# Two engines instead of one for emptying PSUM in a SiLU MLP kernel, with a new row order of x and a regrouped end

## Chip, cores, metric

The kernel runs on one core of a Trainium2 chip. The metric is the device time of one execution in microseconds (us); the times below are of several executions of the same program, and the profile is of one execution.

## The reference

```python
B, S, D, F = 1, 2048, 640, 1728     # all bf16
def reference(x, w1, w2):
    h = jnp.einsum("bsd,df->bsf", x, w1)
    h = _silu(h)                     # h * sigmoid(h)
    out = jnp.einsum("bsf,fd->bsd", h, w2)
    return out
```

Two matrix products with a SiLU between them: 2048 rows of x, 640 wide, are taken to 1728 hidden columns and back to 640.

## The kernel before

**Tiling.** Both products contract over the partitions. The 640 columns of x are five blocks of 128 (`DT`), the 1728 hidden columns are padded to fourteen blocks of 128 (`FT`), and the 2048 rows are four chunks of 512 (`NSC`) in the first product and sixteen tiles of 128 (`ST`) in the second. The kernel is written engine by engine: each engine has its own program, in the order in which it will run, and semaphores tie them together. There is no scheduler; the order is what stands there.

**The start.** The first product needs x transposed, as `xT_sb` (columns of x on partitions). For rows 512 to 2047 a transposing DMA does it (L146). For the first chunk TensorE does it: SP loads four pieces of 128 rows into `x0_sb`, one DMA each (L129), with a semaphore each; TensorE multiplies each 128x128 block with an identity (L198, five matmuls for each piece) into PSUM `ps2`, seen as 128-column slots (`tp_view`); VectorE copies the five blocks of a piece, 640 columns, as one cast into `xT_sb` (L282). PSUM holds two pieces, so the transposes of the third piece wait until VectorE has copied the first (`sem_tpc`, L195). While x is under way, TensorE runs four matmuls on zeros (L184), and ScalarE loads its table with a first Sigmoid on a small tile (L258). SP's queue in order: four x pieces, three groups of w1 (L136; the first of them holds two hidden blocks), then a wait for the first w1 group, then fifteen transposing DMAs with w2's loads among them, then the sixteen stores of the output.

**First product (L223).** For each chunk and each hidden block five matmuls with 512 moving columns go into one of four PSUM buffers `ps1`. ScalarE takes the Sigmoid of it into `sig_sb` (L269), VectorE multiplies the two into `hT_sb` (L292), and that frees the buffer. All 56 blocks run before the second product begins.

**Second product (L246).** For each tile of 128 rows, fourteen hidden blocks, and for each of them two matmuls with the same weights (`hT_sb`): 512 output columns into one PSUM bank and 128 into the next. Every matmul has a weight load of its own. `ps2` holds two tiles, so tile st waits for the evacuation of tile st-2 (`sem_ev2`). VectorE casts the 640 columns of a tile into one of three `o_sb` buffers (L305), and SP stores it (L173). At the end SP waits for the stores (L178).

Of the kernel before, what the change touches and what calls it, by code (L numbers as in the profile page):

```python
# [9 lines left out]
def bass_standalone__dense_activation_silu__prompt_kernel(  # L10
# [11 lines left out]
    S, D = xf.shape  # L22
    F = w1.shape[1]
    P = 128
    assert D % P == 0 and S % 512 == 0
    DT = D // P
    FT = (F + P - 1) // P
    FP = FT * P
# [1 line left out]
    ST = S // P  # L30
# [2 lines left out]
    JB = SCH // P  # L33
    NB1 = 4
    NOB = 3
    d_chunks = []
    d0 = 0
    while d0 < D:
        d1 = min(d0 + 512, D)
        d_chunks.append((d0, d1))  # L40
        d0 = d1

    def msz(ft):
        return P

    w1_groups = [(0, 2), (2, 8), (8, FT)]

# [8 lines left out]
    n_w2_dmas = 3 if n_w2_full != FT else 2  # L56
    N_INIT = 4 if FP != F else 3
    N_WARM_MM = 4

    with ExitStack() as es:  # L60
        def sb(name, shape, dtype):
# [22 lines left out]
        sem_init = sem("sem_init")  # L84
        sem_w2pad = sem("sem_w2pad")
        sem_z = sem("sem_z")
        sem_x0 = [sem(f"sem_x0_{j}") for j in range(JB)]
        sem_x = [None] + [sem(f"sem_x{i}") for i in range(1, NSC)]
        sem_w1 = [sem(f"sem_w1_{i}") for i in range(len(w1_groups))]
        sem_w2 = sem("sem_w2")  # L90
        sem_o = [sem(f"sem_o{i}") for i in range(NOB)]
        sem_tp = sem("sem_tp")
        sem_tpc = sem("sem_tpc")
        sem_pe1 = sem("sem_pe1")
        sem_act1 = sem("sem_act1")
        sem_dve1 = sem("sem_dve1")
        sem_pe2 = sem("sem_pe2")
        sem_ev2 = sem("sem_ev2")
        block = es.enter_context(nc.Block())

        w1_v = w1.rearrange("(dt p) f -> p dt f", p=P)
        w2_full_v = w2[0:n_w2_full * P, :].rearrange("(ft p) d -> p ft d", p=P)

        @block.gpsimd
        def _(pool):
# [18 lines left out]

        @block.sync
        def _(sp):
            x0_v = xf[0:SCH, :].rearrange("(j p) d -> p j d", p=P)
            for j in range(JB):
                sp.dma_start(  # L129
                    out=x0_sb[:, j, :], in_=x0_v[:, j, :]  # L130
                ).then_inc(sem_x0[j], 16)

            def load_w1_group(gi):
                a, b = w1_groups[gi]
                f0, f1 = a * P, min(b * P, F)
                sp.dma_start(  # L136
                    out=w1_sb[:, :, f0:f1], in_=w1_v[:, :, f0:f1]
                ).then_inc(sem_w1[gi], 16)

            for gi in range(len(w1_groups)):  # L140
                load_w1_group(gi)

            def x_chunk_transposes(sc):
                s0 = sc * SCH
                for dt in range(DT):
                    sp.dma_start_transpose(  # L146
                        out=xT_sb[:, dt, s0:s0 + SCH],
                        in_=xf[s0:s0 + SCH, dt * P:(dt + 1) * P],
                    ).then_inc(sem_x[sc], 16)

            sp.wait_ge(sem_w1[0], 16)
            for sc in range(1, NSC):
                x_chunk_transposes(sc)
                if sc == min(2, NSC - 1):
                    sp.dma_start(
                        out=w2_sb[:, 0:w2_half, :], in_=w2_full_v[:, 0:w2_half, :]
                    ).then_inc(sem_w2, 16)
                    sp.dma_start(
                        out=w2_sb[:, w2_half:n_w2_full, :],
                        in_=w2_full_v[:, w2_half:n_w2_full, :],  # L160
                    ).then_inc(sem_w2, 16)
                    sp.wait_ge(sem_w2pad, 1)
                    if n_w2_full != FT:
                        sp.dma_start(
                            out=w2_sb[0:F_LAST, FT - 1, :],
                            in_=w2[n_w2_full * P:F, :],
                        ).then_inc(sem_w2, 16)

            o_cnt = [0] * NOB
            for st in range(ST):  # L170
                ob = st % NOB
                sp.wait_ge(sem_ev2, st + 1)
                sp.dma_start(  # L173
                    out=of[st * P:(st + 1) * P, :], in_=o_sb[:, ob, :]
                ).then_inc(sem_o[ob], 16)
                o_cnt[ob] += 1
            for ob in range(NOB):
                sp.wait_ge(sem_o[ob], 16 * o_cnt[ob])  # L178

        @block.tensor  # L180
        def _(pe):
# [8 lines left out]
                )  # L190
            pe.wait_ge(sem_init, N_INIT)
            for j in range(JB):
                pe.wait_ge(sem_x0[j], 16)
                if j >= 2:
                    pe.wait_ge(sem_tpc, j - 1)  # L195
                base = 8 * (j % 2)
                for dt in range(DT):
                    ins = pe.matmul(  # L198
                        tp_view[:, base + dt, :],
                        lhsT=x0_sb[:, j, dt * P:(dt + 1) * P],  # L200
                        rhs=ident[:, :],
                        start=True,
                        stop=True,
                    )
                ins.then_inc(sem_tp, 1)

            w1_waited = set()
            for sc in range(NSC):
                if sc == 0:
                    pe.wait_ge(sem_tpc, JB)  # L210
                else:
                    pe.wait_ge(sem_x[sc], 16 * DT)
                for ft in range(FT):
                    idx = sc * FT + ft
                    buf = idx % NB1
                    gi = w1_group_of(ft)
                    if gi not in w1_waited:
                        pe.wait_ge(sem_w1[gi], 16)
                        w1_waited.add(gi)
                    if idx >= NB1:  # L220
                        pe.wait_ge(sem_dve1, idx - NB1 + 1)
                    for dt in range(DT):
                        ins = pe.matmul(  # L223
                            ps1[:, buf, :],
                            lhsT=w1_sb[:, dt, ft * P:(ft + 1) * P],
                            rhs=xT_sb[:, dt, sc * SCH:(sc + 1) * SCH],
                            start=(dt == 0),
                            stop=(dt == DT - 1),
                        )
                    ins.then_inc(sem_pe1, 1)  # L230
# [1 line left out]
            pe.wait_ge(sem_w2pad, 1)  # L232
            pe.wait_ge(sem_w2, 16 * n_w2_dmas)
            dve1_waited = 0
            for st in range(ST):
                b2 = st % 2
                sc = (st * P) // SCH
                if st >= 2:
                    pe.wait_ge(sem_ev2, st - 1)
                for ft in range(FT):  # L240
                    idx = sc * FT + ft
                    if dve1_waited < idx + 1:
                        pe.wait_ge(sem_dve1, idx + 1)
                        dve1_waited = idx + 1
                    for ci, (c0, c1) in enumerate(d_chunks):
                        ins = pe.matmul(  # L246
                            ps2[:, b2, ci * 512:ci * 512 + (c1 - c0)],
                            lhsT=hT_sb[:, ft, st * P:(st + 1) * P],
                            rhs=w2_sb[:, ft, c0:c1],
                            start=(ft == 0),  # L250
                            stop=(ft == FT - 1),
                        )
                ins.then_inc(sem_pe2, 1)

        @block.scalar
        def _(act):
            act.wait_ge(sem_init, N_INIT)
            act.activation(  # L258
                out=warm_sb[:, :], in_=warm_sb[:, :], func=ACT.Sigmoid
            )  # L260
            for sc in range(NSC):
                for ft in range(FT):
                    idx = sc * FT + ft
                    buf = idx % NB1
                    m = msz(ft)
                    act.wait_ge(sem_pe1, idx + 1)
                    if idx >= NB1:
                        act.wait_ge(sem_dve1, idx - NB1 + 1)
                    act.activation(  # L269
                        out=sig_sb[0:m, buf, :],  # L270
                        in_=ps1[0:m, buf, :],
                        func=ACT.Sigmoid,
                    ).then_inc(sem_act1, 1)

        @block.vector
        def _(dve):
            dve.memset(z_sb[:, :], 0.0).then_inc(sem_z, 1)  # L277
            dve.wait_ge(sem_init, N_INIT)
            for j in range(JB):
                base = 8 * (j % 2)  # L280
                dve.wait_ge(sem_tp, j + 1)
                dve.tensor_copy(  # L282
                    out=xT_sb[:, :, j * P:(j + 1) * P],
                    in_=tp_view[:, base:base + DT, :],
                ).then_inc(sem_tpc, 1)
            for sc in range(NSC):
                for ft in range(FT):
                    idx = sc * FT + ft
                    buf = idx % NB1
                    m = msz(ft)  # L290
                    dve.wait_ge(sem_act1, idx + 1)
                    dve.tensor_tensor(  # L292
                        out=hT_sb[0:m, ft, sc * SCH:(sc + 1) * SCH],
                        in0=ps1[0:m, buf, :],
                        in1=sig_sb[0:m, buf, :],
                        op=ALU.mult,
                    ).then_inc(sem_dve1, 1)
            o_cnt = [0] * NOB
            for st in range(ST):
                b2 = st % 2  # L300
                ob = st % NOB
                dve.wait_ge(sem_pe2, st + 1)
                if o_cnt[ob] > 0:
                    dve.wait_ge(sem_o[ob], 16 * o_cnt[ob])
                dve.tensor_copy(  # L305
                    out=o_sb[:, ob, :], in_=ps2[:, b2, 0:D]
                ).then_inc(sem_ev2, 1)
                o_cnt[ob] += 1


# [26 lines left out]
```

## Time and profile before

| | |
|---|---|
| Median of 6 runs | 135.99 us (134.99 to 136.43) |
| Profiled execution | 136.62 us |
| its span, first to last instruction | 134.7 us |
| First product on the chain (L223) | 46.8% of the span |
| Second product on the chain (L246) | 44.8% |
| DMA of the first w1 group on the chain | 3.5% |
| Issues of the x pieces on the chain (L129) | 1.2% |
| Last evacuation on the chain (L305) | 0.6% |

The span is shorter than the execution's time by 1.9 us, which lie before the first and after the last instruction. In the profile PE is TensorE's matmuls, PEld its weight loads, DVE VectorE, ACT ScalarE, POOL GpSimd, SP the engine that issues all DMAs here; L129 is line 129 of the kernel. The chain is followed back from the last instruction: at each step to what released it, or else to the instruction before it on its engine. In a group of instructions stand how often it ran, its busy time in us, the mean length of one in ns, then how long the engine was idle just before such an instruction and what ended that. In a timeline the first column is the start from the beginning of the span, the second the time until the end of the group, both in us. Some matmul records are missing from a trace.

### The profile page before, as it was taken

Reading aid. Unit: us, or ns where it says so; the run is one execution under the profiler, and the core shown is the slowest. Engines: PE = TensorE matmul, PEld = TensorE weight load, DVE = VectorE, ACT = ScalarE, POOL = GpSimd, SP = SyncE. Lnnn points to the kernel's source line nnn. Section 1 sums busy time; section 2 is a strip of 40 time slices with the busy share of each in tenths; the row PEclk is TensorE's granted clock in tenths of the full one; section 3 lists DMA queues with packets and bytes.
Section 4 is the critical chain, followed back from the end, with each engine's and each line's share of the span. In section 5 each row is a group of like instructions: output and inputs, shape, how many; then the busy total and the mean of one; then the engine's idle time right before and its main releaser. Section 6 shows DMA issues by size and latency. Waiting matters only on the chain.

```text
span 134.7 us, 1780 instructions
## 1 busy us (share of the span) xinstructions
PE 127.9 (95%) x737; PEld 64.8 (48%) x752; DVE 55.2 (41%) x77; ACT 35.0 (26%) x58; POOL 1.6 (1%) x9
## 2 busy tenths in 40 slices
PE   5779999999999999999999999999999999999990
PEld 1523444444444444444445555555555555555550
DVE  0714566666666666666663222221112222221122
ACT  4002555555555555555551000000000000000000
POOL 4000000000000000000000000000000000000000
PEclk9999999999999999999999999999999999999999
DMA  3999446997000000000000110011111110111111
GB/s 114 286 356 233 106 107 164 379 206 147 0 0 0 2 5 0 2 0 0 0 0 0 54 49 25 24 49 54 49 49 49 49 54 14 35 49 49 53 49 49
DMA packets 14792, 9.78 MB, mean 73 GB/s; under 512 B 8576, under 2 KB 14784, under 8 KB 14784
## 3 DMA queue, kind: packets, MB, share of 16 engines
q1 hardware_dynamic: 14784, 9.67, 26.8%
q8 instruction: 6, 0.10, 0.4%
q14 instruction: 2, 0.02, 0.0%
HBM read 5.08 MB, written 2.62 MB: 57 GB/s over the span
## 4 chain that ended last, share of the span: by engine, by line
PE 92%; DMA 4%; SPq 1%; issue 1%; DVE 1%
PE ps L223 47%; PE ps L246 45%; DMA w_sb<-in_w_dram 4%; SPq L129 1%; DVE o_sb L305 1%
## 5 line engine op out<-in xcount | busy, mean ns | idle before, releaser
L223 PE MATMUL ps<-xT_sb,w_sb 128*128 128x512 bf16 x274 | 63.0, 391 | 1.4 <-DMA w_sb<-in_w_dram 1.1
L246 PE MATMUL ps<-w_sb,hT_sb 128*128 128x512 bf16 (+1 forms) x439 | 60.5, 297 | 0.5
L292 DVE TENSOR_TENSOR hT_sb<-ps,sig_sb 128x512 bf16<-128x512 f32 x56 | 38.7, 690 | 26.2 <-ACT sig_sb L269 26.2
L246 PEld LDWEIGHTS ps<-w_sb,hT_sb 128*128 128x128 bf16 x448 | 34.5, 98 | 26.6
L223 PEld LDWEIGHTS ps<-xT_sb,w_sb 128*128 128x128 bf16 x280 | 28.0, 100 | 36.2 <-issue 3.6
L269 ACT ACTIVATE sig_sb<-ps 128x512 bf16<-128x512 f32 x56 | 33.4, 597 | 35.7 <-PE ps L223 35.7
L305 DVE CAST o_sb<-ps 128x640 bf16<-128x640 f32 x16 | 13.2, 825 | 47.2 <-PE ps L246 47.2
L282 DVE CAST xT_sb<-ps 128x640 bf16<-128x640 f32 x4 | 3.1, 820 | 3.0 <-PE ps L198 2.9
L198 PE MATMUL ps<-ident,x_sb 128*128 128x128 bf16 x20 | 2.6, 305 | 0.7 <-DVE xT_sb L282 0.5
L184 PE MATMUL ps<-z_sb 128*128 128x512 bf16 x4 | 1.9, 628 | 1.2 <-DVE z_sb L277 1.2
L198 PEld LDWEIGHTS ps<-ident,x_sb 128*128 128x128 bf16 x20 | 1.9, 135 | 2.1 <-issue 1.3
L258 ACT ACT_TABLE_LOAD x1 | 1.3, 1283 | 0.7 <-PEq L322 0.7
L184 PEld LDWEIGHTS ps<-z_sb 128*128 128x128 bf16 x4 | 0.4, 130 | 1.7 <-DVE z_sb L277 1.2
L121 POOL MEMSET w_sb<- 128x640 bf16 x1 | 0.6, 633 | 0.0
L277 DVE MEMSET z_sb<- 128x256 uint32 x1 | 0.3, 272 | 0.9 <-PEq L322 0.9
L118 POOL MEMSET w_sb<- 128x320 bf16 x1 | 0.4, 367 | 0.0
L108 POOL TENSOR_SCALAR_AFFINE_SELECT ident<-ident 128x128 bf16<-128x128 bf16 x1 | 0.3, 294 | 0.2 <-POOL ident L106 0.2
L258 ACT ACTIVATE warm_sb<-warm_sb 128x32 f32<-128x32 f32 x1 | 0.2, 229 | 0.0
L106 POOL MEMSET ident<- 128x128 bf16 x1 | 0.2, 205 | 0.3 <-POOLq L322 0.3
L119 POOL MEMSET warm_sb<- 128x32 f32 x1 | 0.1, 127 | 0.0
L322 POOL MEMSET const-bfloat16-1.0<- 128x1 bf16 x1 | 0.1, 102 | 0.0
L322 POOL MEMSET const-uint8-127<- 128x1 uint8 x1 | 0.1, 102 | 0.0
(2 smaller groups left out, 0.2 us busy)
## 6 DMA issues: line engine op xcount, KB each, us to landing
out_dram<-o_sb SPq DMA_DIRECT2D x16, 160.0 KB, 1.8
w_sb<-in_w_dram SPq DMA_DIRECT2D x2, 960.0 KB, 6.2
w_sb<-in_w_dram SPq DMA_DIRECT2D x1, 1120.0 KB, 9.3
w_sb<-in_w_dram SPq DMA_DIRECT2D x1, 880.0 KB, 8.6
x_sb<-in_x_dram SPq DMA_DIRECT2D x4, 160.0 KB, 2.6
w_sb<-in_w_dram SPq DMA_DIRECT2D x1, 320.0 KB, 4.7
xT_sb<-in_x_dram SPq DMA_TRANSPOSE x15, 3.5
w_sb<-in_w_dram SPq DMA_DIRECT2D x1, 80.0 KB, 8.9
```

Source lines behind the costliest of these rows:

```text
L118: pool.memset(w1_sb[:, :, F:FP], 0.0).then_inc(sem_init, 1)
L121: pool.memset(w2_sb[:, FT - 1, :], 0.0).then_inc(sem_w2pad, 1)
L129: sp.dma_start(out=x0_sb[:, j, :], in_=x0_v[:, j, :]).then_inc(sem_x0[j], 16)
L184: pe.matmul(ps1[:, NB1 - 1, :], lhsT=z_sb[:, 0:P], rhs=z_sb[:, :], start=True, stop=True,)
L198: ins = pe.matmul(tp_view[:, base + dt, :], lhsT=x0_sb[:, j, dt * P:(dt + 1) * P], rhs=ident[:, :], start=True, stop=True,)
L223: ins = pe.matmul(ps1[:, buf, :], lhsT=w1_sb[:, dt, ft * P:(ft + 1) * P], rhs=xT_sb[:, dt, sc * SCH:(sc + 1) * SCH], start=(dt == 0), stop ...
L246: ins = pe.matmul(ps2[:, b2, ci * 512:ci * 512 + (c1 - c0)], lhsT=hT_sb[:, ft, st * P:(st + 1) * P], rhs=w2_sb[:, ft, c0:c1], start=(ft == 0),
L258: act.activation(out=warm_sb[:, :], in_=warm_sb[:, :], func=ACT.Sigmoid)
L269: act.activation(out=sig_sb[0:m, buf, :], in_=ps1[0:m, buf, :], func=ACT.Sigmoid,).then_inc(sem_act1, 1)
L282: dve.tensor_copy(out=xT_sb[:, :, j * P:(j + 1) * P], in_=tp_view[:, base:base + DT, :],).then_inc(sem_tpc, 1)
L292: dve.tensor_tensor(out=hT_sb[0:m, ft, sc * SCH:(sc + 1) * SCH], in0=ps1[0:m, buf, :], in1=sig_sb[0:m, buf, :], op=ALU.mult,).then_inc(sem ...
L305: dve.tensor_copy(out=o_sb[:, ob, :], in_=ps2[:, b2, 0:D]).then_inc(sem_ev2, 1)
```

## The change

Four things are changed together.

- *x pieces.* Two DMAs of two rows a partition each instead of four of one: row 4p+j of the chunk is now on partition p in piece j, so one DMA reads two neighbouring rows (2560 bytes) for each partition.
- *Transposes.* The five blocks of a piece lie in two PSUM banks, three and two. VectorE copies three (384 columns), ScalarE two (256 columns), each into every fourth column of `xT_sb`, which restores the order of the rows. The semaphore `sem_tpc` becomes two, and TensorE waits for both.
- *Output evacuation.* VectorE copies columns 0 to 511 of a tile, ScalarE columns 512 to 639, each with its own semaphore; TensorE and SP wait for both.
- *The last two tiles.* Their matmuls are regrouped: first both tiles' 512-column halves, 28 matmuls into the two banks of one buffer, then both tiles' 128-column parts, 28 matmuls into the two banks of the other. Each group's evacuations begin when the whole group is done, and each part has its own store: four stores in place of two.

```diff
+    DA = 512
+    DB = D - DA
...
+    TPV = 3
+    def tp_slot(j, dt):
+        base = 8 * (j % 2)
+        return base + dt if dt < TPV else base + 4 + (dt - TPV)
...
+        segs = []
+        for st in range(ST - 2):
+            b2 = st % 2
+            segs.append([(st, 0, b2, 0, DA), (st, 1, b2, DA, DB)])
+        sA, sB = ST - 2, ST - 1
+        segs.append([(sA, 0, 0, 0, DA), (sB, 0, 0, 512, DA)])
+        segs.append([(sA, 1, 1, 0, DB), (sB, 1, 1, 512, DB)])
...
-            x0_v = xf[0:SCH, :].rearrange("(j p) d -> p j d", p=P)
-            for j in range(JB):
-                sp.dma_start(
-                    out=x0_sb[:, j, :], in_=x0_v[:, j, :]
-                ).then_inc(sem_x0[j], 16)
+            x0_v = xf[0:SCH, :].rearrange("(p j) d -> p j d", j=JB)
+            hj = JB // 2
+            sp.dma_start(out=x0_sb[:, 0:hj, :], in_=x0_v[:, 0:hj, :]).then_inc(
+                sem_x0[0], 16
+            )
+            sp.dma_start(out=x0_sb[:, hj:JB, :], in_=x0_v[:, hj:JB, :]).then_inc(
+                sem_x0[1], 16
+            )
...
-            for st in range(ST):
+            for st in range(ST - 2):
                 ob = st % NOB
-                sp.wait_ge(sem_ev2, st + 1)
+                sp.wait_ge(sem_ev_v, st + 1)
+                sp.wait_ge(sem_ev_a, st + 1)
                 sp.dma_start(
                     out=of[st * P:(st + 1) * P, :], in_=o_sb[:, ob, :]
+                ).then_inc(sem_o[ob], 16)
+                o_cnt[ob] += 1
+            for st in (sA, sB):
+                ob = st % NOB
+                sp.wait_ge(sem_ev_v, st + 1)
+                sp.dma_start(
+                    out=of[st * P:(st + 1) * P, 0:DA], in_=o_sb[:, ob, 0:DA]
+                ).then_inc(sem_o[ob], 16)
+                o_cnt[ob] += 1
+            for st in (sA, sB):
+                ob = st % NOB
+                sp.wait_ge(sem_ev_a, st + 1)
+                sp.dma_start(
+                    out=of[st * P:(st + 1) * P, DA:D], in_=o_sb[:, ob, DA:D]
                 ).then_inc(sem_o[ob], 16)
...
             for j in range(JB):
-                pe.wait_ge(sem_x0[j], 16)
+                if j == 0:
+                    pe.wait_ge(sem_x0[0], 16)
+                if j == JB // 2:
+                    pe.wait_ge(sem_x0[1], 16)
                 if j >= 2:
-                    pe.wait_ge(sem_tpc, j - 1)
+                    pe.wait_ge(sem_tpc_v, j - 1)
+                    pe.wait_ge(sem_tpc_a, j - 1)
                 for dt in range(DT):
                     ins = pe.matmul(
-                        tp_view[:, base + dt, :],
+                        tp_view[:, tp_slot(j, dt), :],
...
+                for (st, ci, b2, c0, ncol) in seg:
+                    sc = (st * P) // SCH
+                    idx_need = sc * FT + FT
+                    if dve1_waited < idx_need:
+                        pe.wait_ge(sem_dve1, idx_need)
+                        dve1_waited = idx_need
                 for ft in range(FT):
-                    for ci, (c0, c1) in enumerate(d_chunks):
+                    for (st, ci, b2, c0, ncol) in seg:
+                        d0 = 0 if ci == 0 else DA
                         ins = pe.matmul(
-                            ps2[:, b2, ci * 512:ci * 512 + (c1 - c0)],
+                            ps2[:, b2, c0:c0 + ncol],
                             lhsT=hT_sb[:, ft, st * P:(st + 1) * P],
-                            rhs=w2_sb[:, ft, c0:c1],
+                            rhs=w2_sb[:, ft, d0:d0 + ncol],
...
+            for j in range(JB):
+                s0_ = tp_slot(j, TPV)
+                act.wait_ge(sem_tp, j + 1)
+                act.copy(
+                    out=xT_sb[:, TPV:DT, j:SCH:JB],
+                    in_=tp_view[:, s0_:s0_ + (DT - TPV), :],
+                ).then_inc(sem_tpc_a, 1)
...
+            for st in range(ST):
+                ob = st % NOB
+                b2, c0, ncol = grp_loc[(st, 1)]
+                act.wait_ge(sem_pe2, seg_done_idx[(st, 1)])
+                if o_cnt[ob] > 0:
+                    act.wait_ge(sem_o[ob], 16 * o_cnt[ob])
+                act.copy(
+                    out=o_sb[:, ob, DA:D], in_=ps2[:, b2, c0:c0 + ncol]
+                ).then_inc(sem_ev_a, 1)
...
                 dve.tensor_copy(
-                    out=xT_sb[:, :, j * P:(j + 1) * P],
-                    in_=tp_view[:, base:base + DT, :],
-                ).then_inc(sem_tpc, 1)
+                    out=xT_sb[:, 0:TPV, j:SCH:JB],
+                    in_=tp_view[:, s0_:s0_ + TPV, :],
+                ).then_inc(sem_tpc_v, 1)
...
                 dve.tensor_copy(
-                    out=o_sb[:, ob, :], in_=ps2[:, b2, 0:D]
-                ).then_inc(sem_ev2, 1)
+                    out=o_sb[:, ob, 0:DA], in_=ps2[:, b2, c0:c0 + ncol]
+                ).then_inc(sem_ev_v, 1)
```

## The prediction, made before the result was known

> **What bounds the kernel now.** I read the page's busy table and its chain first, then the chain in order of time, the groups of instructions by shape, and the timelines of the first 8 us and of the last 4.
>
> ```profile
> PE 127.9 (95%) x737; PEld 64.8 (48%) x752; DVE 55.2 (41%) x77; ACT 35.0 (26%) x58; POOL 1.6 (1%) x9
> ...
> PE 92%; DMA 4%; SPq 1%; issue 1%; DVE 1%
> ```
>
> TensorE carries 92% of the chain, so what is off TensorE's path is worth nothing. Only three stretches are not plain matmul streaming: the start, the last evacuation, and the last store.
>
> ```profile
> 0.74 0.40 SPq L129
> ...
> 2.13 0.43 SPq L129
> ...
> 2.61 4.74 DMA w_sb<-in_w_dram
> 7.35 0.14 issue
> 7.48 8.29 PE ps L223 x25
> ```
>
> The start, as the chain has it: four x loads are issued one behind another (L129), the first w1 group only at 2.61, it lands at 7.35, and the main loop starts at 7.48. But a second path ends beside it:
>
> ```profile
> 3.24 1.23 PE L198 MATMUL ps<-ident,x_sb 128*128 128x128 bf16 x10 [0.16 <-DMA x_sb<-in_x_dram]
> 4.04 3.25 DVE L282 CAST xT_sb<-ps 128x640 bf16<-128x640 f32 x4 [2.90 <-PE ps L198]
> ...
> 5.01 1.42 PE L198 MATMUL ps<-ident,x_sb 128*128 128x128 bf16 x10 [0.55 <-DVE xT_sb L282]
> ```
>
> VectorE's four evacuations run almost without a pause from 4.04 to 7.29, 0.06 before the w1 group lands. Whoever shortens one of the two gates gains 0.06; this change touches both.
>
> ```profile
> L292 DVE TENSOR_TENSOR hT_sb<-ps,sig_sb 128x512 bf16<-128x512 f32 x56 | 38.7, 690 | 26.2 <-ACT sig_sb L269 26.2
> L246 PEld LDWEIGHTS ps<-w_sb,hT_sb 128*128 128x128 bf16 x448 | 34.5, 98 | 26.6
> ...
> L269 ACT ACTIVATE sig_sb<-ps 128x512 bf16<-128x512 f32 x56 | 33.4, 597 | 35.7 <-PE ps L223 35.7
> L305 DVE CAST o_sb<-ps 128x640 bf16<-128x640 f32 x16 | 13.2, 825 | 47.2 <-PE ps L246 47.2
> L282 DVE CAST xT_sb<-ps 128x640 bf16<-128x640 f32 x4 | 3.1, 820 | 3.0 <-PE ps L198 2.9
> L198 PE MATMUL ps<-ident,x_sb 128*128 128x128 bf16 x20 | 2.6, 305 | 0.7 <-DVE xT_sb L282 0.5 <-DMA x_sb<-in_x_dram 0.2
> ```
>
> Of the sixteen output evacuations (L305) nobody appears as waiting for one: TensorE needs a buffer again one tile (3.8 us) after its evacuation begins. Only the last one is on the path.
>
> **Prices of the new instructions.** VectorE: 640 columns take 822 ns (L282, L305), 512 take 690 (L292, another operation), so 1.03 ns a column; 384 columns come to 558 ns, 512 to 690. In a finer timeline the first two casts take 1.55 together where one lasts 0.82, so they start 0.73 apart, and casts of 384 columns 0.47. ScalarE: 512 columns 597 ns, and the warm-up's 32 columns 229 (L258), so 0.77 ns a column; 256 columns 401 ns, 128 columns 303.
>
> **The start, part by part.** *Two x loads instead of four.* SP issues each in about 0.46 (0.74 to 2.61 for four), so the w1 group is issued 0.93 earlier, at 1.68. If its landing follows, the gate is at 6.42; if the bytes ahead of it decide, it stays at 7.35. I take something below 7.0, because the issue spacing is what the chain shows, and keep 7.35 as the other end. *Later first x.* The first transposes now wait for twice the bytes. Before, the second piece was issued 0.46 after the first and its matmuls followed without a gap, so the first transpose moves from 3.24 to 3.69 (ends: 3.24, and 3.75 by 164 KB at the 323 GB/s that the DMA moved from 2.5 to 3.0). *Split evacuation.* VectorE started 0.80 after the first transpose matmul (3.24 to 4.04); now at 4.49, and 384 columns end at 5.05. ScalarE's 256 end at 4.89, never the later of the two. Ten transposes of 0.31 take 1.23, so they start 0.10 apart and the second tile is 0.51 behind: VectorE 5.00 to 5.56. The third tile's transposes need the first tile's buffer (5.05, and 0.15 to the matmul as from 4.86 to 5.01) and the second x load: the DMA had moved 663 KB, all of x's chunk, by 4.5, and the first piece landed some 0.6 after its bytes, so 5.1. Start 5.2; VectorE 0.73 later (as from 5.01 to 5.74, the last two casts being 1.55 before 7.29): 5.93 to 6.49. Fourth tile: transposes at 5.71, when the second tile's buffer is free and the third's are through; VectorE 6.44 to 7.00, main loop 0.15 later: **7.15 instead of 7.48, -0.33**. Ends: 0 if the w1 gate stays; -0.78 if the first half of x lands as early as the first quarter did and the second half does not hold (the chain 0.45 earlier, 6.70).
>
> *Strided stores.* Row 4p+j now sits on partition p, so the evacuations write every fourth column of xT_sb. No row stores with a step. Nearest is L282 itself, at 1.03 ns a column with steps between its five blocks; I take that. The upper end doubles the time per column: VectorE 0.96 a tile and 0.87 apart; first tile 4.49 to 5.45, second to 6.32, fourth tile's transposes then at 6.47, its evacuation 7.2 to 8.16, main loop 8.31: +0.83. A gain is excluded: the columns are the same.
>
> *Waits.* Transposes now wait for two engines; ScalarE is done 0.16 earlier. ScalarE's copies stand ahead of its first Sigmoid, which came at 9.81; they end near 6.85 (401 ns from 6.44). Should Copy need another table load (1.28, L258), it fits between 2.26 and 4.49, and the way back before the first Sigmoid; without that cover 1.28. The chunk transposes (L146) wait for the w1 group and move with it; the second chunk's five are issued by about 13.8 (half of the ten's 12.94 after 7.37) and land 3.5 later, and are wanted at 25.3 (57 matmuls of 0.216 after 12.98).
>
> **The clock.** The granted clock reads 1.00 throughout, yet the rows show a slow start:
>
> ```profile
> 11.71 0.15 PEld L223 LDWEIGHTS ps<-xT_sb,w_sb 128*128 128x128 bf16 x1 [0.28 <-issue]
> 12.13 0.15 PEld L223 LDWEIGHTS ps<-xT_sb,w_sb 128*128 128x128 bf16 x1 [0.28 <-issue]
> 12.98 10.93 PEld L223 LDWEIGHTS ps<-xT_sb,w_sb 128*128 128x128 bf16 x51 [0.28 <-issue]
> ```
>
> 0.43 us a matmul until 12.98, then 10.93/51 = 0.214. If the moment of that step is fixed, a main loop 0.33 earlier saves only half, 0.16, for the extra work before the step runs at half rate; if it moves with the loop, 0.33. I take 0.33. The six runs spread over 1.44 us, which is what a step that wanders by 2.9 us would do; half a microsecond is thus near the noise.
> The Trainium skill ("TensorE: Matmul & The Clock Gate", What's actually happening) has a free-running window of about 3.4 us that must be busy before the full clock: here the step came 5.5 us after the loop began, which that allows. By it the saving is on average the whole 0.33, in one run anything from -1.4 to +2.0.
>
> **Output phase.** Each tile is evacuated by VectorE (512 columns, 690 ns) and ScalarE (128, 303 ns) side by side instead of 825 ns. Hidden by a tile's 3.80 us of matmuls; 0. TensorE's extra wait per tile asks for evacuations over 2.5 us old; 0, and if each cost an "issue" piece of the chain (0.05), 0.7 over fourteen. The wait for the hidden activations (sem_dve1) now names a whole chunk's fourteen at once; the last of all ends at 72.2, and TensorE reads that chunk from 116 on: 0.
>
> *Last two tiles regrouped.* First 28 matmuls of 512 columns, then 28 of 128. In the chain 50 of L223 (49 records, the missing one, a 0.05 piece) take 10.79, so 0.216 each; 50 alternating ones of L246 take 6.79, a pair 0.272, so a 128-column matmul costs 0.056. If the order does not matter, 7.61 as before. The other end: 98 ns of weight load for each of the 28 in the open, 2.74 instead of 1.57, +1.18. I take 0, since in L198 weight loads of 0.147 stand beside consecutive 128-column matmuls that start 0.10 apart, so they are hidden even there. A gain is excluded, for the columns are the same.
> Against the change speaks the Trainium skill ("TensorE: Matmul & The Clock Gate", Back-to-back issue gap): about 81 ns a matmul at 128 columns in a stream with a weight load each. By it the 28 would cost 0.70 more; its 131 ns for 512 columns is not what this trace shows (216).
>
> *The tail.*
>
> ```profile
> 131.71 0.82 DVE L305 CAST o_sb<-ps 128x640 bf16<-128x640 f32 x1 [2.98 <-PE ps L246]
> 132.56 0.33 SPq L173 DMA_DIRECT2D out_dram<-o_sb  x1
> ```
>
> Now two ScalarE copies of 128 columns: 131.71 to 132.01 and to 132.31. SP issues four stores instead of two; the two of 512 columns go out during the 128-column matmuls (VectorE done 1.4 after the first group, the second group lasts 1.57). The two narrow ones at 132.04 and, after the first's 0.33, 132.40: 0.16 earlier than 132.56. A store took 1.8 to land; 32 KB instead of 160 saves up to 0.39 (128 KB at 323 GB/s) or nothing, since a row is now 256 bytes. I take 0.10. **Tail -0.26**, from 0 to -0.55.
>
> **Sum.** -0.33 - 0.26 = -0.59. The profiled execution took 136.62 (span 134.70 and 1.92 around it), so 136.03 there; it stands 0.63 above the median of the runs. From the median, 135.99 - 0.59 = **135.4**.
>
> **Rivals.** (1) *The w1 gate stays at 7.35*: two loads fewer, but the same bytes ahead of it (655 KB of x). For: the DMA was 0.71 to 0.94 busy from 2 to 5 us. Against: the chain puts the issues on the path. The main loop stays at 7.48: 135.99 - 0.26 = 135.7. (2) *Everything early*: first x as before and a quick narrow store: 135.99 - 0.78 - 0.55 = 134.7. For: the first piece's landing holds much fixed time (2.4 us for 0.5 us of bytes). Against: the DMA's rate in that stretch. (3) *The strided stores are slow*: xT_sb becomes the gate. It decides from about 0.7 us a tile on VectorE, where the fourth evacuation ends past 7.3; doubled it gives +0.83: 135.99 + 0.83 - 0.26 = 136.6, beyond that over 137. For: no row with such a step. Against: the values are narrow and the rate is one column at a time already. (4) *Weight loads exposed in the narrow group*: 135.99 - 0.59 + 1.18 = 136.6. For: 98 ns against 56. Against: L198.
>
> **How the numbers follow.** The forecast has 0.42, its own range 134.9 to 135.9; (1) 0.14; (2) 0.16; (3) 0.15; (4) 0.13. A measurement can tell about 0.5%, 0.68 us, so the borders are 135.31 and 136.67. Faster: somewhat under half of the forecast (0.19) and (2): 0.35. Slower: most of (3) and (4), whose prices have more above them through the clock's scatter: 0.18. Within: 0.47. The range, 134.6 to 136.9, takes all centres and leaves out the far ends of (2) and (3).
>
> **What would show it.** First matmul of the main loop near 7.2, with VectorE's last transpose evacuation just before it, casts of 384 columns near 560 ns and ScalarE's near 400; 28 starts 56 ns apart in the last group; the last store issued some 0.7 after the last matmul's release. I am wrong if the evacuations last twice as long, if the main loop waits for the w1 group, if the narrow matmuls stand 80 or more apart, or if the clock's step falls systematically elsewhere.

## The result, and the profile after

| | before | after |
|---|---|---|
| Median, all runs | 135.80 us (134.40 to 136.43, 20 runs) | 136.55 us (136.15 to 137.25, 10 runs) |
| Ratio to before | | 1.0074, 95% interval 1.0039 to 1.0108 |
| Span of the profiled execution | 134.7 us | 135.1 us |
| First matmul of the main loop | 7.48 us | 8.38 us |
| Last evacuation's start to the end of the span | 3.0 us | 2.6 us |

The change made the kernel slower, by 0.6% in the medians and 0.7% by the ratio. The ratio leaves out executions more than 1.5% above a kernel's fastest, which here, where the times scatter by 2 us, also cuts off ordinary ones; so the medians of all runs stand beside it throughout.

The chain of the changed kernel in order of time (start, length, what; both in us) shows the new bound at once:

```profile
0.73 2.96 DMA x_sb<-in_x_dram
3.69 0.14 issue
3.83 0.70 PE ps L243 x5
...
4.63 3.71 DVE xT_sb L360 x4
8.34 0.05 issue
8.38 8.16 PE ps L269 x25
```

Before, the chain went through the issues of the x loads and the first w1 group. Now it goes through the first x load, landing at 3.69, and then through VectorE's four transpose evacuations, 3.71 us of them. The w1 group is no longer on it. The groups say why:

```profile
L382 DVE CAST o_sb<-ps 128x512 bf16<-128x512 f32 x16 | 11.0, 690 | 48.3 <-PE ps L306 48.3
L348 ACT CAST o_sb<-ps 128x128 bf16<-128x128 f32 x16 | 4.1, 265 | 56.5 <-PE ps L306 56.5
L360 DVE CAST xT_sb<-ps 128x384 bf16<-128x384 f32 x4 | 3.7, 1020 | 3.5 <-PE ps L243 3.5
...
L325 ACT CAST xT_sb<-ps 128x256 bf16<-128x256 f32 x4 | 2.7, 733 | 3.0 <-PE ps L243 2.9
```

The output evacuations cost what was expected, 690 and 265 ns. The transpose evacuations do not: 384 columns on VectorE take 1020 ns, longer than the 640 columns before (820), and 256 on ScalarE 733, more than a Sigmoid of 512 (597). These two rows alone store with a step.

The end of the changed kernel in the timeline:

```profile
130.91 1.29 DVE L382 CAST o_sb<-ps 128x512 bf16<-128x512 f32 x2 [5.35 <-PE ps L306]
131.63 0.93 SPq L208 DMA_DIRECT2D out_dram<-o_sb  x2
132.48 0.43 ACT L348 CAST o_sb<-ps 128x128 bf16<-128x128 f32 x2 [7.34 <-PE ps L306]
132.77 0.83 SPq L215 DMA_DIRECT2D out_dram<-o_sb  x2
```

VectorE is released at 130.91, when the 512-column group is done, and ScalarE at 132.48, when the narrow group is: 1.57 us for 28 matmuls, 56 ns each. The order of the matmuls costs nothing (from the first matmul of the second product to the last evacuation both kernels take 60.89 us), and from 132.48 to the end it takes 0.4 us less than from 131.71 before.

The second product begins at 70.82 before and at 71.59 after, as the two chains have it, before's first:

```profile
70.82 6.25 PE ps L246 x46
```

```profile
71.59 6.25 PE ps L306 x46
```

So in the two profiled executions: +0.90 at the start, of which 0.13 is back by the second product, and -0.4 at the end: +0.4 in the span, +0.30 in their times (136.62 and 136.92). The medians differ by 0.75 and the ratio says 1.0. The profiled execution of before lay 0.82 above its median and that of after 0.37, so the other 0.45 lies in executions that left no trace; the experiments look for it.

### The profile page after: what moved, and what is told of

Same layout as the page of the kernel before. It is cut to its first block, busy times and chain, and to the rows that moved or that the text cites. A ratio compares the mean times of both kernels' runs of the same rounds, so it can differ in the third digit from the quotient of the medians.

```text
span 135.1 us, 1839 instructions
## 1 busy us (share of the span) xinstructions
PE 127.8 (95%) x738; PEld 64.8 (48%) x752; DVE 53.6 (40%) x77; ACT 41.8 (31%) x78; POOL 1.6 (1%) x9
## 4 chain that ended last, share of the span: by engine, by line
PE 92%; DVE 3%; DMA 2%; issue 1%; ACTq 0%; ACT 0%; DVEq 0%
PE ps L269 47%; PE ps L306 45%; DVE xT_sb L360 3%; DMA x_sb<-in_x_dram 2%; PE ps L243 1%; ACTq L60 0%; ACT o_sb L348 0%; DVEq L359 0%
## 5 line engine op out<-in xcount | busy, mean ns | idle before, releaser
L382 DVE CAST o_sb<-ps 128x512 bf16<-128x512 f32 x16 | 11.0, 690 | 48.3 <-PE ps L306 48.3
L348 ACT CAST o_sb<-ps 128x128 bf16<-128x128 f32 x16 | 4.1, 265 | 56.5 <-PE ps L306 56.5
L360 DVE CAST xT_sb<-ps 128x384 bf16<-128x384 f32 x4 | 3.7, 1020 | 3.5 <-PE ps L243 3.5
L325 ACT CAST xT_sb<-ps 128x256 bf16<-128x256 f32 x4 | 2.7, 733 | 3.0 <-PE ps L243 2.9
```

The source lines that it names most:

```text
L325: act.copy(out=xT_sb[:, TPV:DT, j:SCH:JB], in_=tp_view[:, s0_:s0_ + (DT - TPV), :],).then_inc(sem_tpc_a, 1)
L348: act.copy(out=o_sb[:, ob, DA:D], in_=ps2[:, b2, c0:c0 + ncol]).then_inc(sem_ev_a, 1)
L360: dve.tensor_copy(out=xT_sb[:, 0:TPV, j:SCH:JB], in_=tp_view[:, s0_:s0_ + TPV, :],).then_inc(sem_tpc_v, 1)
L382: dve.tensor_copy(out=o_sb[:, ob, 0:DA], in_=ps2[:, b2, c0:c0 + ncol]).then_inc(sem_ev_v, 1)
```

## The experiments

Each was timed beside before on the same chip. The figures for before differ by up to 0.5 us between these sets of runs, so kernels of different sets are compared by their distance from the before beside them. The cast is of 384 columns where VectorE and ScalarE share a piece, and of 640 in step alone, end alone and before with fillers. "Main loop" is the first product's first matmul in the profiled execution.

| kernel | median, us (range) | before there | ratio, 95% interval | VectorE's transpose cast, ns | main loop, us |
|---|---|---|---|---|---|
| old rows | 135.23 (134.05 to 136.14) | 135.86 | 0.9965 (0.9928 to 1.0002) | 555 | 8.13 |
| step alone | 138.00 (137.56 to 138.89) | 135.86 | 1.0191 (1.0144 to 1.0237) | 1600 | 9.76 |
| end alone | 134.94 (133.25 to 135.84) | 135.86 | 0.9913 (0.9871 to 0.9956) | 817 | 6.99 |
| rows put back in the store | 135.08 (133.72 to 136.49) | 135.86 | 0.9999 (0.9953 to 1.0045) | 555 | 7.54 |
| step of two | 134.70 (133.01 to 136.07) | 135.36 | 0.9977 (0.9920 to 1.0035) | 581 | 7.02 |
| start alone | 136.70 (136.03 to 137.33) | 135.36 | 1.0137 (1.0071 to 1.0204) | 1020 | 8.30 |
| six warm-up matmuls | 135.47 (134.09 to 135.85) | 135.36 | 1.0017 (0.9968 to 1.0067) | 1036 | 8.19 |
| four loads | 134.59 (133.27 to 136.71) | 135.36 | 0.9958 (0.9909 to 1.0008) | 555 | 6.84 |
| before with fillers | 134.10 (133.68 to 134.84) | 135.55 | 0.9948 (0.9909 to 0.9986) | 820 | 7.31 |
| after with fillers | 134.37 (134.17 to 134.43) | 135.55 | 0.9963 (0.9933 to 0.9992) | 1037 | 8.4 |
| four loads with fillers | 133.70 (133.11 to 134.78) | 135.55 | 0.9929 (0.9884 to 0.9974) | 556 | 8.52 |
| old rows with fillers | 133.43 (132.87 to 134.07) | 135.84 | 0.9898 (0.9857 to 0.9939) | 553 | 7.21 |

### Is it the step of the stores, or the two engines at once?

Old rows: the changed kernel with contiguous stores.

```diff
-            x0_v = xf[0:SCH, :].rearrange("(p j) d -> p j d", j=JB)
+            x0_v = xf[0:SCH, :].rearrange("(j p) d -> p j d", p=P)
...
-                    out=xT_sb[:, TPV:DT, j:SCH:JB],
+                    out=xT_sb[:, TPV:DT, j * P:(j + 1) * P],
...
-                    out=xT_sb[:, 0:TPV, j:SCH:JB],
+                    out=xT_sb[:, 0:TPV, j * P:(j + 1) * P],
```

> The changed kernel with the old order of x rows (row j*128+p on partition p), so that both engines store contiguous columns; everything else as changed. Theory S (a 2-byte store with a step of four columns costs about 2.2 ns a column on either engine instead of 1.03 and 0.77): VectorE's 384-column casts near 560 ns, ScalarE's 256-column ones near 400, main loop's first matmul at 7.1 to 7.5 instead of 8.38, time about 0.9 to 1.0 us below the changed kernel, 135.3 to 135.7. Rival C (the two engines slow each other because they empty PSUM into the same tile at the same time): casts stay at about 1020 and 730, main loop stays near 8.3, time near 136.5.

Step alone: the kernel before with the stepped store on VectorE alone.

```diff
-            x0_v = xf[0:SCH, :].rearrange("(j p) d -> p j d", p=P)
+            x0_v = xf[0:SCH, :].rearrange("(p j) d -> p j d", j=JB)
...
-                    out=xT_sb[:, :, j * P:(j + 1) * P],
+                    out=xT_sb[:, :, j:SCH:JB],
```

> The kernel before with one thing of the change: row 4p+j on partition p and VectorE's 640-column casts written with a step of four columns; four x loads, VectorE alone. Theory S: each cast 163 + 640 x 2.2 = about 1570 ns, the four follow one another from about 4.0, main loop near 10.1, time 2.6 us above before, about 138.4. Rival C: casts at 820 as before, main loop at 7.5, time as before, 135.8.

The timeline of old rows:

```profile
3.85 1.23 PE L243 MATMUL ps<-ident,x_sb 128*128 128x128 bf16 x10 [0.78 <-DMA x_sb<-in_x_dram]
4.58 0.37 ACT L325 CAST xT_sb<-ps 128x256 bf16<-128x256 f32 x1 [2.32 <-PE ps L243]
4.66 1.02 DVE L360 CAST xT_sb<-ps 128x384 bf16<-128x384 f32 x2 [3.53 <-PE ps L243]
...
6.05 1.09 DVE L360 CAST xT_sb<-ps 128x384 bf16<-128x384 f32 x2 [0.37 <-PE ps L243]
...
8.13 1.44 PE L269 MATMUL ps<-xT_sb,w_sb 128*128 128x512 bf16 x3 [1.59 <-DMA w_sb<-in_w_dram]
```

The group of step alone:

```profile
L282 DVE CAST xT_sb<-ps 128x640 bf16<-128x640 f32 x4 | 5.8, 1600 | 2.8 <-PE ps L198 2.8
```

Both kernels speak for the step, and the rival, two engines that slow each other, falls. Without the step the engines run side by side at 555 and 372 ns; with it VectorE alone takes 1600 ns (1570 expected) and before becomes 2.1 us slower in the median (2.6 expected; the main loop began at 9.76, not 10.1). The expectation on the main loop of old rows failed: xT_sb was complete at 7.14, yet the loop began at 8.13, because in this execution the first w1 group landed only at 8.0. That gate is taken up below.

### Does any step cost?

Step of two: two neighbouring rows on a partition in each load, not four.

```diff
-            x0_v = xf[0:SCH, :].rearrange("(p j) d -> p j d", j=JB)
+            x0_v = xf[0:SCH, :].rearrange("(h p j) d -> p h j d", p=P, j=2)
...
-                    out=xT_sb[:, 0:TPV, j:SCH:JB],
+                    out=xT_sb[:, 0:TPV, (j // 2) * 256 + j % 2:(j // 2) * 256 + 256:2],
...
```

> The changed kernel with a step of two columns instead of four (two neighbouring rows for each partition and x load; loads still of 2560 bytes a partition). Theory S1 (the price is of any store that isn't contiguous, about 2.2 ns a column): casts stay at about 1020 and 730 ns, main loop near 8.3, time 136.3 to 136.8. Rival S2 (the price grows with the step: 1.03 at one, 2.2 at four): casts of 384 columns between 560 and 800 and ScalarE's between 370 and 550, main loop 7.4 to 7.8, time 135.1 to 135.9.

```profile
L360 DVE CAST xT_sb<-ps 128x384 bf16<-128x384 f32 x4 | 2.2, 581 | 3.7 <-PE ps L243 3.7
...
L325 ACT CAST xT_sb<-ps 128x256 bf16<-128x256 f32 x4 | 1.8, 444 | 2.8 <-PE ps L243 2.6
```

The price grows with the step. Taking off the fixed part (163 ns on VectorE, and 158 on ScalarE from its 372 and 265 ns at 256 and 128 columns), a column costs VectorE 1.02, 1.09 and 2.23 ns at steps of one, two and four, and ScalarE 0.84, 1.12 and 2.25. At four the two engines, of different speed otherwise, cost the same. A step of two keeps the loads of 2560 bytes, its casts are nearly as short as contiguous ones, and the kernel is at 134.70 beside 135.36 for before, where the step of four is above before. The casts are where the second theory had them; main loop and time came out lower than either theory said, with a w1 group that landed at 5.5 in this execution.

### The rows put back elsewhere

Contiguous stores, columns left in the order 4p+j, and the first four output tiles written to rows 4p+j:

```diff
+                if st < JB:
+                    dst = of[0:SCH, :].rearrange("(p j) d -> p j d", j=JB)[:, st, :]
+                else:
+                    dst = of[st * P:(st + 1) * P, :]
...
```

> The changed kernel with the new order of x rows kept through: contiguous stores into xT_sb (columns stay in the order 4p+j), and the first four output tiles' stores put the rows back (rows 4p+j, 1280 bytes each). Theory S: casts near 560 and 400 ns, main loop 7.2 to 7.5, time 135.3 to 135.7, as the one with old rows within 0.3; the stepped output rows cost nothing. Rival C: casts stay at 1020 and 730, time near 136.5.

The casts take 555 ns as expected. The median is 135.08, a little under the expected range and within 0.15 of old rows, and the main loop waits for the w1 group until 7.54. The reordering can be had in the output's stores for nothing that shows.

### The parts alone

End alone: the start of before (x loads, waits, one 640-column cast), the changed kernel's output phase.

```diff
...
-                if j == 0:
-                    pe.wait_ge(sem_x0[0], 16)
-                if j == JB // 2:
-                    pe.wait_ge(sem_x0[1], 16)
+                pe.wait_ge(sem_x0[j], 16)
...
-                    out=xT_sb[:, 0:TPV, j:SCH:JB],
-                    in_=tp_view[:, s0_:s0_ + TPV, :],
+                    out=xT_sb[:, :, j * P:(j + 1) * P],
+                    in_=tp_view[:, s0_:s0_ + DT, :],
...
```

> The kernel before with the change's output phase alone (split evacuation, regrouped last two tiles, four stores); start as before. From the two traces the stretch from the last matmul's start to the end of the span is 0.41 us shorter and the narrow matmuls stand 56 ns apart: 135.8 - 0.4 = 135.4. If the regrouped matmuls or the extra waits cost something that I overlooked, 135.8 or more.

Start alone: the reverse, before's output phase with the changed start.

```diff
...
-                dve.tensor_copy(
-                    out=xT_sb[:, :, j * P:(j + 1) * P],
-                    in_=tp_view[:, base:base + DT, :],
-                ).then_inc(sem_tpc, 1)
+                dve.tensor_copy(
+                    out=xT_sb[:, 0:TPV, j:SCH:JB],
+                    in_=tp_view[:, s0_:s0_ + TPV, :],
+                ).then_inc(sem_tpc_v, 1)
...
```

> The kernel before with the change's start alone (two x loads, split transposes evacuation with step four); output phase as before. If start and end add up: the changed kernel's 136.55 plus what the end alone gained (0.4 by the traces, 0.9 by the medians): 136.95 to 137.45, main loop near 8.4. If the end's gain in the medians was partly the clock's luck, nearer 136.95.

The end alone is faster (134.94 against 135.86, 0.4 of which the traces explain), the start alone slower (136.70 against 135.36): -0.9 and +1.3 in the medians, together +0.4, beside +0.75 for the whole change. The start alone lies under its expected 136.95, as before lay 0.4 lower in that set of runs than with the changed kernel. That the end gains 0.9 in the medians and 0.4 in the traces is probably scatter of the start; no run separates it. The profile of end alone shows where scatter of that size can come from:

```profile
4.89 0.44 PE L236 MATMUL ps<-ident,x_sb 128*128 128x128 bf16 x5 [0.55 <-DVE xT_sb L345]
...
6.99 1.84 PEld L261 LDWEIGHTS ps<-xT_sb,w_sb 128*128 128x128 bf16 x10 [1.10 <-DVE xT_sb L345]
6.99 2.33 PE L261 MATMUL ps<-xT_sb,w_sb 128*128 128x512 bf16 x10 [0.93 <-DVE xT_sb L345]
```

Ten matmuls in 2.33 us: here TensorE ran at 0.22 us a matmul from the first, with a start that is before's, and five transposes in 0.44 us say that it was fast already at 4.89. In the profiles of before and after the first twelve or thirteen took 0.43 each.

### When does TensorE become fast?

In the profile of after:

```profile
3.83 1.22 PE L243 MATMUL ps<-ident,x_sb 128*128 128x128 bf16 x10 [0.75 <-DMA x_sb<-in_x_dram]
...
5.74 1.53 PE L243 MATMUL ps<-ident,x_sb 128*128 128x128 bf16 x10 [0.69 <-DVE xT_sb L360]
...
8.38 5.79 PE L269 MATMUL ps<-xT_sb,w_sb 128*128 128x512 bf16 x14 [1.12 <-DVE xT_sb L360]
```

TensorE stands idle from the end of the warm-up to 3.83 (before: 3.24), then before 5.74 and before 8.38, and the main loop's first 14 matmuls take 5.79 us. The Trainium skill ("TensorE: Matmul & The Clock Gate", What's actually happening) has a window of about 3.4 us of activity ahead of the fast state; a longer idle stretch may spoil more positions of it. How long a stretch such a window bears no run here measures. Two extra matmuls on zeros close the first stretch alone:

```diff
-    N_WARM_MM = 4
+    N_WARM_MM = 6
```

> The changed kernel with six matmuls on zeros at the start instead of four, so that TensorE is busy from 1.19 to 3.75 and not idle from 2.9 to 3.8 while it waits for the first x load; nothing else. Theory K (the later first x leaves TensorE idle and takes away the early clock step that some runs of before have): some runs 1.5 us or more below the changed kernel's lowest (136.15), median 0.3 to 1.0 lower, 135.5 to 136.3. Rival (the step follows only the main loop): times as the changed kernel's, 136.15 to 137.25, median near 136.5.

```profile
2.44 1.49 PE L226 MATMUL ps<-z_sb 128*128 128x512 bf16 x3
...
5.68 0.48 PE L243 MATMUL ps<-ident,x_sb 128*128 128x128 bf16 x5 [0.69 <-DVE xT_sb L360]
...
8.19 2.70 PEld L269 LDWEIGHTS ps<-xT_sb,w_sb 128*128 128x128 bf16 x14 [1.42 <-DVE xT_sb L360]
8.19 2.98 PE L269 MATMUL ps<-xT_sb,w_sb 128*128 128x512 bf16 x13 [1.25 <-DVE xT_sb L360]
```

The main loop begins 0.19 earlier than in after, and its first 13 matmuls take 2.98 us. The distance from the before beside it falls from +0.75 to +0.11 in the medians, and of these 0.64 the earlier main loop is 0.19: some 0.45 is left for the slow matmuls. Four of the twelve runs lie at 134.1 to 134.2, where none of after's was below 136.15 and none of start alone's, which ran in the same set, below 136.03. The rival falls: in this profile five transposes in 0.48 us at 5.68 are fast before the main loop begins. Before with six warm-up matmuls was not run, so how much of this before would gain too is open.

Then all idle stretches are filled, in before and after alike, with matmuls on zeros of 128 columns into a buffer that is overwritten later (`n` after the warm-up and after each piece):

```diff
+            def fill(n):
+                for i in range(n):
+                    pe.matmul(
+                        ps1[:, NB1 - 1, 0:P],
+                        lhsT=z_sb[:, 0:P],
+                        rhs=z_sb[:, 0:P],
+                        start=True,
+                        stop=True,
+                    )
...
```

> The kernel before with 21 matmuls of 128 columns on zeros put into TensorE's idle stretches of the start (3 before the first transposes, 6 after the second piece's, 1 after the third's, 11 after the fourth's); they write a buffer that is overwritten later. Theory K (idle stretches before the main loop decide when the fast cadence begins): the step comes before or near the main loop's start, the 13 slow matmuls go (2.75 us in the profile of before), scatter shrinks to under 1 us, time 133.0 to 133.6. Rival (the step depends on the main loop's own matmuls alone): time as before, 135.0 to 136.4.

> The changed kernel with 32 such matmuls in its idle stretches (9, 8, 3 and 12). With the slow matmuls gone on both sides, what is left against before with fillers is the stepped stores' later main loop (+0.9 in the traces) and the end (-0.4): 0.3 to 0.7 above that kernel, 133.5 to 134.2. If the stepped stores were not the cause of the rest, no difference or -0.4.

The timeline of before with fillers:

```profile
5.74 0.44 PE L211 MATMUL ps<-ident,x_sb 128*128 128x128 bf16 x5
...
7.31 2.33 PE L237 MATMUL ps<-xT_sb,w_sb 128*128 128x512 bf16 x9 [0.51 <-DVE xT_sb L296]
...
9.93 0.98 PEld L237 LDWEIGHTS ps<-xT_sb,w_sb 128*128 128x128 bf16 x6 [0.79 <-DMA w_sb<-in_w_dram]
```

Five transposes in 0.44 at 5.74: the fast cadence is there before the main loop, 4.5 us or less after TensorE became busy for good at 1.19; the window named above allows that. Before falls by 1.45 to 134.10, less than the expected 133.0 to 133.6; after falls from 0.75 above its before to 1.18 under it, and its runs then lie within 0.26 us (those of before with fillers within 1.16, where under 1 was expected). Between the two +0.27 is left of +0.75, a little under the expected +0.3 to +0.7. This does not show that the slow cadence had cost after more than before. The last line says why: with a fast loop from 7.31 TensorE stands before the second w1 group, its weight loads idle for 0.79 until 9.93, which the later loop of after (8.4) does not meet. The first product takes 61.07 us there against 60.60 in after with fillers, so this wait alone, 0.47 in these two executions, is as large as the 0.48 by which the two kernels came closer: it hides a part of the stores' delay.

Fillers with the repaired start, one with four loads and one with two:

> Four x loads, old rows with contiguous split evacuations, the change's end, and 17 such matmuls (3, 6, 0 and 8). The end gives 0.4, a main loop 0 to 0.6 earlier than before's the rest: 0.4 to 1.0 below before with fillers, 132.3 to 133.2, and faster than both kernels.

> The changed kernel with old rows and contiguous stores (two x loads kept) and 24 matmuls on zeros in the idle stretches (9, 6, 0 and 9). Beside the changed kernel with fillers and stepped stores (134.37) only the stores differ. If the later main loop of the stepped stores costs with the slow matmuls gone what the traces with fillers say (main loop 8.4 against about 7.3, less some 0.5 that the second w1 group then holds it): 133.6 to 134.0. If the w1 groups hide it all: 134.2 to 134.5.

Four loads with fillers: 133.70, faster than both kernels but above the expected 132.3 to 133.2. Its timeline has the reason:

```profile
8.52 2.32 PE L277 MATMUL ps<-xT_sb,w_sb 128*128 128x512 bf16 x9 [1.79 <-DMA w_sb<-in_w_dram]
```

TensorE was ready early and waited 1.79 us for the first w1 group in this execution; the early start is given back there. Old rows with fillers is the changed kernel with the old row order and the fillers: 133.43, 0.94 under after with fillers, from which it differs in the rows, the stores and the number of fillers. The two ran in different sets; against the before beside each the distance is 1.23, near the 1.2 by which the main loop begins earlier (7.21 and 8.4). That is more than the 0.4 to 0.8 expected: the w1 groups do not hide the stores' delay here. It is the fastest of all, 1.8% under before and 2.3% under after in the medians.

### The gate that was expected to move

Four loads, old rows and the split evacuations, without fillers:

```diff
-            sp.dma_start(out=x0_sb[:, 0:hj, :], in_=x0_v[:, 0:hj, :]).then_inc(
-                sem_x0[0], 16
-            )
-            sp.dma_start(out=x0_sb[:, hj:JB, :], in_=x0_v[:, hj:JB, :]).then_inc(
-                sem_x0[1], 16
-            )
+            for j in range(JB):
+                sp.dma_start(
+                    out=x0_sb[:, j, :], in_=x0_v[:, j, :]
+                ).then_inc(sem_x0[j], 16)
...
```

> The changed kernel's split evacuations and end, with before's four x loads and old row order, so contiguous stores. Casts 560 and 370 ns; first transpose back at 3.1 to 3.25; xT_sb complete near 6.6. Theory G (the first w1 group lands at 7.1 to 8.0 whatever precedes it and is now the gate): main loop 7.1 to 7.9, waiting for DMA, time 134.7 to 135.2, no better than the end alone. Rival (evacuation was the gate): main loop near 6.8, time 134.3 to 134.6.

The main loop began at 6.84, with the w1 group landed at 6.4, and the median is 134.59. Both numbers are the rival's: in this execution the evacuations were the gate, since the group landed earlier than the first theory had it. Over the profiles its landing scatters: 3.8 to 5.8 us after the issue at 2.6 in the six kernels with four x loads (mean 4.5), 3.9 to 6.2 after the issue at 1.7 in the eight with two (mean 5.3). Issued 0.93 earlier, it lands 0.1 earlier in the mean, near 7.0 either way; with single landings from 5.5 to 8.4, these fourteen executions cannot tell that from a gain of a few tenths. Why one execution has 5.5 and another 8.4 stays open.

## Why the prediction went wrong, by its steps

- **Strided stores: the step that failed.** The prediction took L282's 1.03 ns a column as the nearest row and kept the doubled price as the upper end. The doubled price is what the chip charges: 1020 ns against its 960, main loop 8.38 against its 8.31. L282 steps between its five blocks, but inside a block its columns are neighbours, so it bore on the blocks and not on the step that was new. The step itself cost 1.2 us at the start: old rows, without it, had xT_sb complete at 7.14, near the 7.00 of the prediction, after at 8.34. So -0.33 became +0.90. Rival (3) had the mechanism and 136.6 us; with its 0.15 the weights were the wrong way round. That its number meets the measured 136.55 so closely is in part luck: it was added to 135.99, where before now stands at 135.80, and it had nothing for the slow matmuls. Step alone, old rows and step of two show the cause, and old rows ends 0.63 under the before beside it, where the forecast had 0.59 (in part luck too, for in its profile the w1 group held the main loop until 8.13).
- **The clock: half right, by luck.** In the two profiles the fast cadence came 5.5 and 5.3 us after the main loop's start, so it seemed to move with the loop. In the profiles of the other kernels without fillers it came anywhere from before the loop (end alone, six warm-up matmuls) through 2.0 us after its start (four loads) and 3.8 (old rows) to 5.5. The prediction treated its place as luck, the same for both kernels. The first x load came later as predicted (first transposes at 3.83, just past the upper end of 3.75), and with it a longer idle stretch; when six warm-up matmuls closed it, executions near 134.1 appeared, and the one that was traced has the early step. Size: some 0.45 us of the loss, by the executions without a trace and by the warm-up run, priced at nothing. That before suffers less from it is argued and not shown, for the pair with fillers does not tell it from the wait for w1.
- **The w1 gate: wrong, without effect here.** "Something below 7.0" was taken because the issue was on the chain; it landed at 7.15 in after, and over the profiles the earlier issue brought 0.1 of 0.93 in the mean. Rival (1) was nearer on this. In after the gate is hidden behind the stores.
- **Output phase: right.** 690 and 265 ns, hidden; the additional waits show nowhere on TensorE, whose second product takes 60.89 us before and after.
- **Regrouped last tiles: right.** 28 narrow matmuls in 1.57 us, 56 ns apart with a weight load each. The Trainium skill's 81 ns ("TensorE: Matmul & The Clock Gate", Back-to-back issue gap) was not met; the row of the transposes was the better guide.
- **The tail: right, a little small.** -0.4 against -0.26, inside its bounds.

Sum by measurement: in the traces +0.9 at the start, which is 1.2 for the stores less what the split evacuation brought, 0.13 of it back by the second product, and -0.4 for the end; then 0.45 or so for the slow cadence, by the warm-up run: 0.8, beside 0.75 in the medians and 1.0 in the ratio. The split is no finer than the scatter allows.

## What to carry to other kernels

A row is near to a new operation only if it shares what is new in it: a price for contiguous stores says nothing of a step of four, and here the reordering could be moved to the output's DMA for nothing that shows. A load made larger to save issues delays its first user (the first transposes came at 3.83, not 3.24), and idle time of TensorE before the main loop can be paid twice, as delay and as slow matmuls after it. Filling the start's idle stretches with matmuls on zeros was worth more here (1.45 us for before) than any other single step (0.9 for the end alone).

## What the hardware showed that was not expected

A cast with 2-byte results 8 bytes apart costs 2.23 ns a column on VectorE and 2.25 on ScalarE, at 4 bytes apart 1.09 and 1.12, and contiguous 1.02 and 0.84. From 4 to 8 bytes the price doubles on both engines; below that it hardly moves on VectorE. Other steps were not run, and why it is so stays open. The profile's granted clock reads 1.00 in all slices of before and after while matmuls of 512 columns stand 0.43 us apart; the cadence alone tells the state.
